# One operand for the last 16 keys of a head pair, eight theta matmuls for the last 64 tokens, and their copies on ScalarE

## Chip, cores and metric

The kernel runs on one core of a Trainium2 chip. The metric is the device time of one execution in microseconds; the median of several runs is quoted, and one further execution was taken with the hardware profiler.

## What is computed

The reference has three stages over a batch of 8, with 8 heads, 576 tokens and 64 dimensions a head (512 channels). The first is attention with keys and values averaged over groups of 8 tokens, so 72 keys a head. The second mixes tokens with a rotation by theta = x @ w_theta and ends with a channel step. The third is an ordinary token and channel MLP.

```python
k_p = k.reshape(B, H, Sp, pool, D).mean(axis=3)      # Sp = 72, pool = 8
v_p = v.reshape(B, H, Sp, pool, D).mean(axis=3)
attn = softmax(scale * q @ k_p.T)
x = attn @ v_p                                       # heads side by side: [8, 576, 512]
theta = x @ w_theta
y = w_tok_r @ (x * cos(theta)) + w_tok_i @ (x * sin(theta))
u = x + y
x = u + relu(u @ w_ch)
# then two MLPs, over tokens (256 wide) and over channels (1536 wide)
```

## The kernel before

**Precision.** Matrix products run on `F32R` operands. A value that must keep its precision is split in a high part (`h`, rounded to F32R) and a low part (`l`, the rest), and a product is the sum of high x high, low x high and high x low. `HL3` (L61) lists the three.

**Loops.** The first half of the kernel goes through the batches. While TensorE does the token mix of batch `b` (`mix_steps`, 72 steps of three matmuls each, results `m`), the work of batch `b + 1` is woven in: scores (`emit_sc`), normalisation (`emit_norm`), transposes of the probabilities (`emit_pt`), attention times value (`emit_av`), theta of the first half of the channels and of the last 64 tokens (`emit_theta`), and the products with cosine and sine (`emit_z`). `interleave` (L793) places each of these pieces at a due time from the table `P`, on a clock `clk` that adds up the columns of the matmuls emitted so far; `later` delays the work of VectorE and ScalarE behind a matmul on the same clock. So fewer matmuls in the woven part move the due pieces to an earlier place among the main matmuls. After that a list scheduler settles the order on each engine. Batch 0 goes through a plain fp32 path of its own in `emit_av` and `emit_theta`; batches 1 to 7 go through the split path.

**Last 16 keys.** A head pair has 2 x 72 keys. 128 of them go through `pt` and `vbh`/`vbl`. The 8 that are left of each head, 64 over all heads, are collected in `pl`, transposed once for all pairs (`emit_pt` with p = 4) and kept in `t1`: rows 0 to 63 high, rows 64 to 127 low. Their values are masked to the head pair: `vlh` holds the high values for both row halves, `vll` the low values for rows 0 to 63 and zeros below. So a pair and a stretch of tokens (256 or 320, `TH`) takes five matmuls in `emit_av` (L635): three with `pt`, one with `vlh` and one with `vll`.

**Last 64 tokens.** Theta of tokens 512 to 575 is computed once for cosine and sine: `dup_tail` (L535) copies the last 64 columns of `Xh`, `Xl` and `R` behind themselves on VectorE, and the 128 columns 512 to 639 are the stationary operand of 12 matmuls of 512 columns (`emit_theta` with g = 2, L696). Rows 64 to 127 of the result give the sine, rows 0 to 63 the cosine. One ScalarE activation adds a large constant that rounds (`magic`), VectorE takes the fraction (L718), ScalarE evaluates the sine, and the product goes to `zt`.

**Buffers.** `emit_theta` takes PSUM banks `t0` and `t1` by turns, and the working tiles `tmp0` and `tmp1` by turns; the tail, group 0 and group 1 of theta follow each other, so the tail and group 1 share a working tile and a bank. Attention times value uses four banks `x`, the token mix two banks `m`, freed by the addition into `R` (L789).

**Raw values.** `load_vl` (L389) brings the values of the last keys into both halves of `vlr` in two DMAs, and `prep_vl` (L427) sums over 8 tokens on VectorE, rounds on ScalarE, and builds `vlh` and `vll` on POOL. Batch 1 gets them in `pool_vl` by a matmul instead.

Of the kernel before, what the change touches and what calls it, by code (L numbers as in the profile page):

```python
# [64 lines left out]
def tile_attn_moe(  # L65
# [109 lines left out]
    con = st("con", [128, 136], F32)  # L175
    ident = con[:, 0:128]
    mask = con[:, 128:136]
    magic = st("magic", [128, 1], F32)
# [175 lines left out]
    vlh = st("vlh", [128, 4, 2, 64], F32R)  # L354
# [8 lines left out]
    def open_vlo():  # L363
        vlo["b"] = st("vbl", [128, 4, 128], F32R)
        vlo["l"] = st("vll", [128, 4, 2, 64], F32R)
        for t in vlo.values():
            nc.gpsimd.memset(t.bitcast(F32), 0.0)
# [59 lines left out]
    def prep_vl(b):  # L427
        vr = vlr_t.pop(b)
        vs = st("vls", [128, 64], F32)
        vh = st("vlsh", [128, 64], F32R)  # L430
# [4 lines left out]
        m3 = mask.unsqueeze(2)  # L435

        def fin():
            nc.gpsimd.tensor_sub(out=vs, in0=vs, in1=vh.bitcast(F32))
            nc.gpsimd.tensor_tensor(
                out=vlh.rearrange("p a e d -> p (a e) d"),  # L440
                in0=m3.to_broadcast([128, 8, 64]),
                in1=vh.bitcast(F32).unsqueeze(1).to_broadcast([128, 8, 64]),
                op=ALU.mult,
            )
            nc.gpsimd.tensor_tensor(
                out=vlo["l"][0:64].rearrange("p a e d -> p (a e) d"),
                in0=m3[0:64].to_broadcast([64, 8, 64]),
                in1=vs[0:64].unsqueeze(1).to_broadcast([64, 8, 64]),
                op=ALU.mult,
            )  # L450

        fin()
# [54 lines left out]
    def pool_vl(b):  # L507
# [5 lines left out]
        def masked(o, pr):  # L513
            nc.vector.tensor_tensor(
                out=o[pr].rearrange("p a e d -> p (a e) d"), in0=v[pr],
                in1=mask[pr].unsqueeze(2).to_broadcast([64, 8, 64]), op=ALU.mult,
            )

        lo, up = slice(0, 64), slice(64, 128)
        if b == 0:  # L520
            masked(vl0, lo)
            return
        tm = st("kr", [128, 4, 2, 64], F32, "vlt")
        vll = vlo["l"]
        masked(tm, lo)
        masked(vlh, up)
        nc.scalar.copy(out=vlh[lo], in_=tm[lo])
        nc.gpsimd.tensor_sub(out=vll[lo], in0=tm[lo], in1=vlh[lo].bitcast(F32))
# [9 lines left out]
    def emit_sc(b, p):  # L538
        q = q_t[b, p // 2][:, p % 2, :]
        if p == 0:  # L540
            e_t[b] = st("e", [128, 5, 8, 72], F32)
            pl_t[b] = st("pl", [128, 5, 2, 8, 8], F32)
# [17 lines left out]
    def emit_norm(b, p):  # L560
# [11 lines left out]
        for h in range(2):  # L572
            left = e[:, :, 2 * p + h, 64 * h:64 * h + 8]
            nc.gpsimd.tensor_copy(
                out=pl_t[b][:, :, :, 2 * p + h, :],
# [3 lines left out]
    def emit_pt(b, p):  # L579
# [4 lines left out]
        else:  # L584
            pt = st("t1", [128, T], F32R if b else F32)
            t1_t[b] = pt
        for c0, c1 in ((0, 2), (2, 5)):
# [3 lines left out]
            for c in range(c0, c1):  # L591
                if p < 4:
                    src = e[:, c, 2 * p:2 * p + 2, :].rearrange("p h k -> p (h k)")[:, 8:136]
                else:
                    src = pl_t[b][:, c].rearrange("p a h k -> p (a h k)")
# [3 lines left out]
            if b == 0:  # L599
                o, i = (pt[:, t0:t0 + n], ps[:, 0:n]) if p < 4 else (pt[0:64, t0:t0 + n], ps[0:64, 0:n])  # L600
                (nc.scalar.copy if c0 else nc.vector.tensor_copy)(out=o, in_=i)
# [12 lines left out]
    xh = {}  # L614

    def emit_av(b, j, th):
        t0, n = TH[th]
        ts = slice(t0, t0 + n)
        if j == 0 and th == 0:
            r_t[b] = st(f"R{b % 2}", [128, 4, TD], F32)  # L620
            if b > 0:
                xh[b] = (st("Xh", [128, 4, TD], F32R), st("Xl", [128, 4, TD], F32R))
        need(f"pt{j % 2}", "t1", "vbl")
# [1036 lines left out]
```

## Time and profile before

| | us |
|---|---|
| median of 3 runs (1312.93 to 1313.25) | 1313.01 |
| profiled execution | 1310.61 |
| its span on the core | 1308.7 |
| TensorE matmuls busy | 1262.2 |
| VectorE busy | 970.5 |
| ScalarE busy | 637.1 |
| POOL busy | 325.8 |

The span runs from the first to the last instruction of the profiled execution. Busy times of TensorE count pipelined matmuls with their modelled ends, so the distance between two starts is what one of them takes from the engine. The prologue fills the first 105 us or so; then the batches follow at about 60 us each until 545 us; the channel step and the two MLPs take the rest.

### The profile page before, as it was taken

To read this page: it belongs to the slowest core of one execution; us is meant where nothing else is said; L and a number is where in the kernel's file an instruction comes from. 1 tells how busy PE (TensorE), PEld (TensorE's weight loads), DVE (VectorE), ACT (ScalarE), POOL (GpSimd) and SP (SyncE) were. 2 spreads that over 40 slices of the span, in tenths; PEclk is the share of its full clock that TensorE was granted. 3 is DMA by queue.
4 is the path that set the end of the run, shared out by engine and by line. 5 is a ranking of instruction groups with operands and counts; after the bars stand their busy time and mean duration, and the time that the engine had idled before them with its cause. 6 is when DMAs were issued, how large, how long until landed. Compare 5 with 4: busy or idle time off the path is not lost.

```text
span 1308.7 us, 22307 instructions
## 1 busy us (share of the span) xinstructions
PE 1262.2 (96%) x8216; PEld 1211.6 (93%) x8216; DVE 970.5 (74%) x1749; ACT 637.1 (49%) x1190; POOL 325.8 (25%) x340
## 2 busy tenths in 40 slices
PE   6899999999999998999999999999999999999998
PEld 3588999999999998999999998999999999999998
DVE  7988576675859598587765778897555499988894
ACT  4775455545555645243332346665445454444442
POOL 4653324242324244211110002320000031223122
PEclk9999999999999999999999999999999999999999
DMA  9423221222212123446684278885437976557621
GB/s 337 148 79 115 68 95 68 96 80 84 94 61 75 35 74 125 134 171 221 236 300 182 98 262 296 279 278 195 145 134 244 357 259 224 155 159 223 184 95 66
DMA packets 119612, 213.70 MB, mean 163 GB/s; under 512 B 11152, under 2 KB 65936, under 8 KB 119504
## 3 DMA queue, kind: packets, MB, share of 16 engines
q1 hardware_dynamic: 119504, 212.29, 48.3%
q8 instruction: 64, 1.05, 0.3%
q14 instruction: 44, 0.36, 0.1%
HBM read 133.60 MB, written 78.64 MB: 162 GB/s over the span
## 4 chain that ended last, share of the span: by engine, by line
PE 69%; DVE 20%; DMA 3%; issue 3%; ACT 2%; POOL 1%; SPq 0%; DVEq 0%; ACTq 0%; POOLq 0%
PE x L159 25%; PE m L159 21%; PE t L159 20%; PE x L173 2%; DVE sm L564 2%; DVE e L553 2%; DVE mx L552 2%; DVE tmp L736 1%; DVE sm L565 1%; DMA ws<-w_ch 1%; DVE pt L605 1%; DVE R L789 1%; DVE early L261 1%; DMA scr_x<-u 1%; DVE sums L398 1%
## 5 line engine op out<-in xcount | busy, mean ns | idle before, releaser
L159 PE MATMUL m<-wtk,Z 128*128 128x256 f32 (+1 forms) x1536 | 245.0, 298 | 8.4 <-DVE R L789 6.4
L159 PEld LDWEIGHTS m<-wtk,Z 128*128 128x128 f32 x1536 | 216.0, 188 | 11.5 <-DVE R L789 6.6
L751 POOL TENSOR_TENSOR Z<-tmp,Z 128x1024 fp32r<-128x1024 f32 x31 | 76.3, 2462 | 109.4 <-ACT Z L750 109.4
L159 PE MATMUL x<-ope_Z,wa 128*128 128x384 f32 x492 | 94.8, 336 | 0.0
L1382 POOL TENSOR_TENSOR o<-o,u 128x384 f32<-128x384 f32 x12 | 16.3, 1382 | 286.1 <-DVE u L1370 195.7
L159 PEld LDWEIGHTS x<-ope_Z,wa 128*128 128x128 f32 x492 | 86.3, 188 | 0.1
L1016 POOL TENSOR_TENSOR wsum<-wm 128x128 f32<-128x128 f32 (+1 forms) x18 | 15.1, 837 | 270.0 <-DVE wm L1006 262.4
L159 PE MATMUL t<-wth,Xh 128*128 128x256 f32 (+1 forms) x504 | 76.3, 293 | 0.5 <-DVE Xh L536 0.2
L159 PEld LDWEIGHTS t<-wth,Xh 128*128 128x128 f32 x504 | 66.9, 188 | 4.5 <-DVE Xh L536 1.8
L718 DVE SCALAR_TENSOR_TENSOR tmp<-tmp,t 128x512 f32<-128x512 f32 x40 | 27.3, 683 | 53.5 <-ACT tmp L705 53.5
L736 DVE TENSOR_TENSOR tmp<-x,tmp 128x1024 f32<-128x1024 f32 x32 | 39.1, 1220 | 31.2 <-ACT tmp L712 16.1
L159 PE MATMUL x<-bdk,q 128*128 128x144 f32 x320 | 47.8, 303 | 11.6 <-DVE bdk L1441 7.1
L159 PEld LDWEIGHTS x<-bdk,q 128*128 128x128 f32 x320 | 44.7, 204 | 13.9 <-issue 11.2
L159 PE MATMUL m<-wtk,zt 128*128 128x256 f32 (+1 forms) x192 | 56.6, 295 | 0.0
L705 ACT ACTIVATE tmp<-t,magic 128x512 f32<-128x512 f32 x40 | 27.3, 683 | 54.6 <-PE t L159 42.9
L569 POOL TENSOR_TENSOR e<-e,sm 128x720 f32<-128x720 f32 x32 | 45.0, 1406 | 31.6 <-DVE sm L568 31.1
L558 ACT ACTIVATE e<-e 128x720 f32<-128x720 f32 x32 | 25.7, 804 | 51.1 <-DVE e L553 51.0
L159 PE MATMUL t<-ope_Z,wa 128*128 128x384 f32 x234 | 48.1, 336 | 1.9 <-ACT p L1290 1.9
L789 DVE TENSOR_TENSOR R<-m,R 128x256 f32<-128x256 f32 (+1 forms) x64 | 28.7, 450 | 26.8 <-PE m L159 26.8
L159 PE MATMUL m<-ope_Z,wa 128*128 128x384 f32 x234 | 48.0, 336 | 0.0
L159 PE MATMUL x<-ope_R,wa 128*128 128x384 f32 x228 | 44.1, 338 | 0.3 <-DVE p L1295 0.2
L159 PE MATMUL t<-wth,Xl 128*128 128x256 f32 (+1 forms) x252 | 43.4, 294 | 0.0
(401 smaller groups left out, 3545.3 us busy)
## 6 DMA issues: line engine op xcount, KB each, us to landing
wa<-scr_w SPq DMA_DIRECT2D x42, 512.0 KB, 5.4
scr_g<-g SPq DMA_DIRECT2D x108, 192.0 KB, 2.9
scr_w<-wo SPq DMA_DIRECT2D x42, 256.0 KB, 3.0
scr_u<-R SPq DMA_DIRECT2D x32, 288.0 KB, 2.1
u<-scr_u SPq DMA_DIRECT2D x32, 288.0 KB, 3.9
scr_w<-wo SPq DMA_DIRECT2D x18, 512.0 KB, 3.4
scr_x<-u SPq DMA_DIRECT2D x32, 288.0 KB, 2.1
raw_n<-scr_x SPq DMA_DIRECT2D x24, 384.0 KB, 3.8
```

The lines of the kernel that those rows point to most:

```text
L159: nc.tensor.matmul(out=o, lhsT=l, rhs=r, start=start, stop=stop, skip_group_check=skip)
L173: nc.tensor.transpose(o, i, ident)
L552: nc.vector.tensor_reduce(out=mx[:, c0:c1, :], in_=v, axis=AX.X, op=ALU.max)
L553: nc.vector.tensor_tensor(out=e[:, c0:c1, 2 * p:2 * p + 2, :], in0=v, in1=mx[:, c0:c1, :].unsqueeze(3).to_broadcast([128, n, 2, 72]), op=A ...
L558: nc.scalar.activation(out=ep, in_=ep, func=ACTF.Exp, scale=1.0 / 64.0)
L564: nc.vector.tensor_reduce(out=sm, in_=ep, axis=AX.X, op=ALU.add)
L569: nc.gpsimd.tensor_tensor(out=ep, in0=ep, in1=sm.unsqueeze(3).to_broadcast([128, 5, 2, 72]), op=ALU.mult)
L705: nc.scalar.activation(out=t, in_=pt, func=ACTF.Identity, bias=magic[:, 0:1])
L718: nc.vector.scalar_tensor_tensor(out=t, in0=t, scalar=MAGIC, in1=pt, op0=ALU.subtract, op1=ALU.subtract)
L736: nc.vector.tensor_tensor(out=tmp, in0=px.unsqueeze(1).to_broadcast([128, 2, 512]), in1=tmp, op=ALU.mult)
L751: later(1.0 if lo is nc.vector else 0.0, lambda: lo.tensor_sub(out=zl, in0=zv, in1=zh.bitcast(F32)), tg, zg)
L789: nc.vector.tensor_add(out=R[:, j, ts], in0=o, in1=R[:, j, ts])
```

## The change

**Last 16 keys.** The 64 rows of the last keys are cut in two groups of 32 (head pairs 0 and 1, pairs 2 and 3). For each group a tile of 96 rows holds probabilities as high, high, low, and a tile of values as high, low, high, so that one matmul with 96 rows makes the sum of all three products. `t1` becomes two tiles (`t1` and `n1`), each filled by a ScalarE copy of 64 rows and a VectorE subtraction of 32; `pl` is collected in the matching order; `vlh` becomes the one tile `vlt`, `vll` is used for batch 0 alone, and the masks get eight more columns. The values are loaded in 32-row pieces, three for each group, into `vlr` and `n2`.

**Last 64 tokens.** The high and the low part of the last 64 tokens stand side by side in one stationary operand `xt` (tag `n3`): its first 64 columns give high x w, its last 64 low x w. Eight matmuls (high and low part of w, four slices each) replace 12; the product of low with low is in the sum too. `fold` then adds the lower half of the rows to the upper: ScalarE copies rows 64 to 127 out, VectorE adds, and rounding and fraction go on for 64 rows only.

**Copies.** The duplicate of `R` and the two copies into `xt` run on ScalarE; the duplicates of `Xh` and `Xl` are gone.

```diff
@@ load_vl
-        t = st("vlr", [128, 512], F32)
-        nc.sync.dma_start(out=t[0:64], in_=vl[b])
-        nc.sync.dma_start(out=t[64:128], in_=vl[b])
+        t = [st(x, [128, 512], F32, "vlr") for x in ("vlr", "n2")]
+        for g in range(2):
+            for r in range(3):
+                nc.sync.dma_start(out=t[g][32 * r:32 * r + 32], in_=vl[b, 32 * g:32 * g + 32])
@@ prep_vl
-        nc.vector.tensor_reduce(
-            out=vs, in_=vr.rearrange("p (d o) -> p d o", o=8), axis=AX.X, op=ALU.add
-        )
-        nc.scalar.copy(out=vh, in_=vs)
...
+        for g in range(2):
+            nc.vector.tensor_reduce(
+                out=vs[0:96, g], in_=vr[g][0:96].rearrange("p (d o) -> p d o", o=8), axis=AX.X, op=ALU.add
+            )
+        nc.scalar.copy(out=vh[0:96], in_=vs[0:96])
+        nc.gpsimd.tensor_sub(out=vh[32:64], in0=vs[32:64], in1=vh[32:64].bitcast(F32))
...
@@ emit_pt, p = 4
-                nc.scalar.copy(out=pt[:, t0:t0 + n], in_=ps[:, 0:n])
-                lo = pt[64:128, t0:t0 + n]
-                later(P["lo"], lambda o=lo, i=ps[64:128, 0:n]: nc.vector.tensor_sub(
-                    out=o, in0=i, in1=o.bitcast(F32)), last_bank[0], "t1")
+                for g in range(2):
+                    gr = slice(64 * g, 64 * g + 32)
+                    nc.scalar.copy(out=pt[g][0:64, t0:t0 + n], in_=ps[64 * g:64 * g + 64, 0:n])
+                    later(P["lo"], lambda o=pt[g][64:96, t0:t0 + n], i=ps[gr, 0:n], h=pt[g][0:32, t0:t0 + n]:
+                          nc.vector.tensor_sub(out=o, in0=i, in1=h.bitcast(F32)),
+                          last_bank[0], ("t1", "n1")[g])
@@ emit_av
-            (vlh[:, j].rearrange("p e d -> p (e d)"), t1[:, ts]),
-            (vlo["l"][:, j].rearrange("p e d -> p (e d)"), t1[:, ts]),
+            (vlt[0:96, j].rearrange("p e d -> p (e d)"), t1[j // 2][0:96, ts]),
...
-                dup_tail(h)
-                dup_tail(l)
-                dup_tail(r)
+                for a, x in enumerate((h, l)):
+                    nc.scalar.copy(out=xt[b][:, :, a], in_=x[:, :, 512:T].bitcast(F32))
+                dup_tail(r, nc.scalar.copy)
@@ emit_theta
+            if tail:
+                for w in range(2):
+                    for k in range(4):
+                        mm(o, xt[b][:, k].rearrange("p a t -> p (a t)"), wth[k][:, w, d0:d0 + nd],
+                           n == 0, n == 7)
+                        n += 1
+                continue
...
+        if tail:
+            lo = tmp[0:64, 0, :]
+            nc.scalar.copy(out=lo, in_=pt[64:128])
+
+            def fold():
+                th = tmp[64:128, 0, :]
+                nc.vector.tensor_add(out=th, in0=pt[0:64], in1=lo)
+                nc.scalar.activation(out=t[64:128], in_=th, func=ACTF.Identity, bias=magic[64:128, 0:1])
+
+                def frac():
+                    nc.vector.scalar_tensor_tensor(
+                        out=t[64:128], in0=t[64:128], scalar=MAGIC, in1=th, op0=ALU.subtract, op1=ALU.subtract
+                    )
+
+                    def sins():
+                        nc.scalar.activation(out=t[0:64], in_=t[64:128], func=ACTF.Abs)
+                        nc.scalar.activation(out=t, in_=t, func=ACTF.Sin, scale=-TWO_PI, bias=phase[:, 1:2])
...
```

**Order on TensorE**, batch 4 beside batch 5, at the first products of attention times value (`x` is the result, `pt` and `t` the probabilities, `m` the token mix). Before:

```order
L159 MATMUL x_3792<-pt_3721,vbh 128x320
L159 MATMUL x_3792<-pt_3721,vbl 128x320
L159 MATMUL x_3784<-t_3769,vlh 128x256
L159 MATMUL x_3784<-t_3769,vll 128x256
L159 MATMUL x_3792<-pt_3721,vbh 128x320
L159 MATMUL m_3762<-wtk_552,Z_3442 128x256
L159 MATMUL x_3792<-t_3769,vlh 128x320
L159 MATMUL x_3792<-t_3769,vll 128x320
L159 MATMUL m_3762<-wtk_559,Z_3442 128x256
```

The same place now:

```order
L159 MATMUL x_3807<-pt_3731,vbl 128x320
L159 MATMUL x_3807<-pt_3731,vbh 128x320
L159 MATMUL m_3772<-wtk_552,Z_3447 128x256
L159 MATMUL x_3800<-t_3779,vlh 128x256
L159 MATMUL m_3772<-wtk_559,Z_3447 128x256
L159 MATMUL m_3772<-wtk_594,zt_3260 128x256
L159 MATMUL x_3818<-pt_3748,vbh 128x256
L159 MATMUL x_3818<-pt_3748,vbl 128x256
L159 MATMUL x_3818<-pt_3748,vbh 128x256
L159 MATMUL x_3818<-t_3779,vlh 128x256
L159 MATMUL x_3807<-t_3779,vlh 128x320
```

The `vll` matmuls are gone, a `vbh` matmul of 320 columns and a main matmul of 256 now stand ahead of the first `t` matmul, and the 320-column `t` matmul stands seven places behind it. Between the last product of attention times value and the theta tail there were three main matmuls of 256 columns and twelve of 320; there are 16 of 320 now. From the first `t` matmul to the tail the new order holds nine more main matmuls of 320 columns (21 for 12) and one fewer of 256 (20 for 21), since the tail's due time is the same and less stands before it.

**Order on ScalarE**, same batches, from the last product of attention times value to the theta tail and group 0 of theta (`t_3929`, `t_3946` are the tail's banks). Before:

```order
L645 CAST Xh<-x_3892 128x320
L646 COPY R_3780<-x_3892 128x320
L424 CAST vbh<-sums 64x2x64
L434 CAST vlsh<-vls 128x64
L705 ACTIVATE tmp_3944<-t_3929,magic 128x512
L714 ACTIVATE tmp_3944<-tmp_3944 64x512
L715 ACT_TABLE_LOAD
```

Now:

```order
L636 CAST Xh<-x_3909 128x320
L637 COPY R_3794<-x_3909 128x320
L644 CAST xt<-Xh 128x4x64
L525 COPY R_3794<-R_3794 128x4x64
L424 CAST vbh<-sums 64x2x64
L644 CAST xt<-Xl 128x4x64
L424 CAST vbh<-sums 64x2x64
L435 CAST vlsh<-vls 96x128
L706 COPY tmp_3957<-t_3946 64x512
L711 ACTIVATE tmp_3957<-tmp_3957,magic 64x512
L719 ACTIVATE tmp_3957<-tmp_3957 64x512
```

The three copies of the last tokens stand behind the last R copy, with a `vbh` cast between them, and the tail's activation has become a copy and an activation with VectorE's addition between the two.

## Rows read from the trace of the kernel before

**Rows 1.** The page's busy times with shares, and the last chain by engine.

```profile
PE 1262.2 (96%) x8216; PEld 1211.6 (93%) x8216; DVE 970.5 (74%) x1749; ACT 637.1 (49%) x1190; POOL 325.8 (25%) x340
...
PE 69%; DVE 20%; DMA 3%; issue 3%; ACT 2%; POOL 1%; SPq 0%; DVEq 0%; ACTq 0%; POOLq 0%
```

**Rows 2.** Stretches: length; busy PE, PEld, DVE, ACT, POOL; clock; DMA share; GB/s.

```profile
304.40:364.50 60.10, 58.76 (x449) 57.30 (x449) 41.41 (x81) 32.38 (x61) 20.64 (x20) 1.00 0.26 84
...
485.00:545.00 60.00, 56.27 (x424) 54.79 (x423) 39.42 (x84) 24.48 (x41) 19.34 (x13) 1.00 0.27 88
```

**Rows 3.** Groups by form: count, busy us, mean ns of one, idle before.

```profile
L159 PE MATMUL x<-t,vll 128*128 128x320 f32 x28 | 8.7, 309 | 0.0
...
L159 PE MATMUL x<-t,vll 128*128 128x256 f32 x28 | 7.9, 281 | 0.0
...
L159 PE MATMUL t<-wth,Xl 128*128 128x512 f32 x28 | 7.5, 390 | 0.0
```

**Rows 4.** Timeline, 355 to 357 us, TensorE: start, length, operation.

```profile
355.82 0.28 PE L159 MATMUL x<-t,vll 128*128 128x256 f32 x1
...
355.94 0.31 PE L159 MATMUL x<-pt,vbh 128*128 128x320 f32 x1
...
356.53 0.31 PE L159 MATMUL x<-t,vll 128*128 128x320 f32 x1
...
356.67 0.71 PE L173 MATMUL x<-con,e 128*128 128x128 f32 x5
```

**Rows 5.** Timeline of TensorE, 306 to 327 us.

```profile
306.37 1.07 PE L159 MATMUL t<-wth,Xl 128*128 128x512 f32 x4
307.27 1.10 PE L159 MATMUL t<-wth,Xh 128*128 128x256 f32 x8
...
326.43 0.86 PE L159 MATMUL m<-wtk,Z 128*128 128x256 f32 x6
```

**Rows 6.** Waits of TensorE, 105 to 560 us: total, times, longest.

```profile
PE m L159 <- DVE R L789: 6.0, 7, 1.5
PE x L159 <- DVE t L610: 2.9, 6, 1.4
```

**Rows 7.** Timeline, 352 to 355 us: making of t1 and its first matmul.

```profile
352.53 0.75 ACT L608 CAST t<-x 128x256 fp32r<-128x256 f32 x2 [1.81 <-PE x L173]
...
353.72 0.83 DVE L610 TENSOR_TENSOR t<-x,t 64x256 fp32r<-64x256 f32 x2
...
354.20 0.39 PE L159 MATMUL x<-t,vlh 128*128 128x256 f32 x1 [0.29 <-DVE t L610]
```

**Rows 8.** Timeline, 362 to 365 us: from the last evacuation to the theta tail.

```profile
362.62 0.41 ACT L645 CAST Xh<-x 128x320 fp32r<-128x320 f32 x1
...
362.94 0.42 ACT L646 COPY R<-x 128x320 f32<-128x320 f32 x1
...
363.80 0.66 DVE L536 CAST Xh<-Xh 128x256 fp32r<-128x256 f32 x1
363.84 0.60 PE L159 MATMUL m<-wtk,Z 128*128 128x320 f32 x3
...
364.52 1.69 PEld L159 LDWEIGHTS t<-wth,Xh 128*128 128x128 f32 x8 [0.34 <-DVE Xh L536]
```

**Rows 9.** Timeline of ScalarE, 307 to 323 us: theta and the high half of Z.

```profile
307.47 0.69 ACT L705 ACTIVATE tmp<-t,magic 128x512 f32<-128x512 f32 x1 [1.19 <-PE t L159]
...
316.73 0.69 ACT L705 ACTIVATE tmp<-t,magic 128x512 f32<-128x512 f32 x1 [1.40 <-POOL zt L751]
...
321.46 1.05 ACT L750 CAST Z<-tmp 128x1024 fp32r<-128x1024 f32 x1 [1.29 <-DVE tmp L736]
```

**Rows 10.** Timeline, 506 to 511 us: the first main matmuls of batch 7.

```profile
506.00 0.48 PE L159 MATMUL m<-wtk,Z 128*128 128x256 f32 x2 [1.53 <-DVE R L789]
...
506.68 4.01 POOL L751 TENSOR_TENSOR Z<-tmp,Z 128x1024 fp32r<-128x1024 f32 x1 [2.95 <-ACT Z L750]
...
510.74 0.50 PE L159 MATMUL m<-wtk,Z 128*128 128x256 f32 x2 [1.76 <-POOL Z L751]
```

More of the change, by code (lines that the diff above doesn't have):

```diff
@@ L364, in open_vlo @@
         vlo["b"] = st("vbl", [128, 4, 128], F32R)
-        vlo["l"] = st("vll", [128, 4, 2, 64], F32R)
-        for t in vlo.values():
-            nc.gpsimd.memset(t.bitcast(F32), 0.0)
+        nc.gpsimd.memset(vlo["b"].bitcast(F32), 0.0)
     q_t = {}
@@ L511, in pool_vl, with masked @@
         v = ps.rearrange("p (h d) -> p h d", h=8)
-        def masked(o, pr):
+        def masked(o, pr, m):
             nc.vector.tensor_tensor(
                 out=o[pr].rearrange("p a e d -> p (a e) d"), in0=v[pr],
-                in1=mask[pr].unsqueeze(2).to_broadcast([64, 8, 64]), op=ALU.mult,
+                in1=m[pr].unsqueeze(2).to_broadcast([pr.stop, 8, 64]), op=ALU.mult,
             )
-        lo, up = slice(0, 64), slice(64, 128)
         if b == 0:
-            masked(vl0, lo)
+            masked(vl0, slice(0, 128), mask0)
             return
         tm = st("kr", [128, 4, 2, 64], F32, "vlt")
[L524 to L528, printed above, removed]
+        masked(tm, slice(0, 96), mask)
+        nc.scalar.copy(out=vlt[0:96], in_=tm[0:96])
+        nc.gpsimd.tensor_sub(out=vlt[32:64], in0=tm[32:64], in1=vlt[32:64].bitcast(F32))
     e_t = {}
@@ L574, in emit_norm @@
             nc.gpsimd.tensor_copy(
-                out=pl_t[b][:, :, :, 2 * p + h, :],
+                out=pl_t[b][:, :, p // 2, :, 2 * (p % 2) + h, :],
                 in_=left.unsqueeze(2).to_broadcast([128, 5, 2, 8]),
@@ L584, in emit_pt @@
         else:
-            pt = st("t1", [128, T], F32R if b else F32)
-            t1_t[b] = pt
+            t1_t[b] = [st(x, [128, T], F32R, "t1") for x in ("t1", "n1")] if b else st("t1", [128, T], F32)
+            pt = t1_t[b]
         for c0, c1 in ((0, 2), (2, 5)):
@@ L599, in emit_pt @@
             if b == 0:
-                o, i = (pt[:, t0:t0 + n], ps[:, 0:n]) if p < 4 else (pt[0:64, t0:t0 + n], ps[0:64, 0:n])
-                (nc.scalar.copy if c0 else nc.vector.tensor_copy)(out=o, in_=i)
+                (nc.scalar.copy if c0 else nc.vector.tensor_copy)(out=pt[:, t0:t0 + n], in_=ps[:, 0:n])
             elif p < 4:
@@ L621, in emit_av @@
             if b > 0:
-                xh[b] = (st("Xh", [128, 4, TD], F32R), st("Xl", [128, 4, TD], F32R))
-        need(f"pt{j % 2}", "t1", "vbl")
+                xh[b] = (st("Xh", [128, 4, T], F32R), st("Xl", [128, 4, T], F32R))
+                xt[b] = st("n3", [128, 4, 2, 64], F32R, "xt")
+        need(f"pt{j % 2}", "t1", "n1", "vbl")
         pt, t1 = pt_t[b, j], t1_t[b]
@@ L679, in emit_theta @@
         else:
-            need("Xl")
+            need("Xl", "n3")
         chunks, d0, nd = theta_geo(half, g)
+        tail = g == 2 and b > 0
         if g < 2:
@@ L704, in emit_theta @@
         t = tmp[:, 1, :]
+        if tail:
[12 more added lines that the diff above has]
+                        nc.scalar.activation(out=t, in_=t, func=ACTF.Sin, scale=-TWO_PI, bias=phase[:, 1:2])
+                    later(P["sn"], sins, tg)
+                later(P["fr"], frac, tg)
+            later(P["sn"], fold, bk, tg)
+            return
         nc.scalar.activation(out=t, in_=pt, func=ACTF.Identity, bias=magic[:, 0:1])
```

42 lines of the change are left out of this document (19 added, 23 removed).

## Prediction

> **What bounds the kernel now.** I read the totals first: TensorE is busy for 96% of the span, and the chain that ended last runs over it for 69% [rows 1]. Then the stretches: one batch of the first half lasts 60.10 us, TensorE is busy for 58.76 of them, VectorE for 41.41 and ScalarE for 32.38, all at a granted clock of 1.00, which is the 2.4 GHz level [rows 2]. The list of waits is short: between 105 and 560 us TensorE waited 6.0 us in seven places for the additions into R and 2.9 us in six for `t1` [rows 6]. So a matmul taken out of a batch should come back almost whole, unless it uncovers a chain on the other engines. The batch turn is where I look for that, because all that the change touches lies there.
>
> **What it removes on TensorE.** In each of the seven batches that go through the split path, attention-times-value loses one matmul of five in each of 8 groups (four of 256 columns, four of 320), and theta of the last 64 tokens loses 4 of 12 matmuls of 512 columns. The busy times by form [rows 3] count pipelined matmuls twice over (281, 309 and 390 ns each), so I price by the distance from one start to the next. The 256-column one holds the engine from 355.82 to 355.94, 0.12 us; the 320-column one from 356.53 to 356.67, 0.14 us [rows 4]. The four `Xl` matmuls of theta hold it from 306.37 to 307.27, 0.90 us or 0.225 each [rows 5].
> - Attention-times-value: 28 x 0.12 + 28 x 0.14 = 7.3 us.
> - Theta: 28 x 0.225 = 6.3 us.
> - Together 13.6 us, 1.94 a batch. The bounds of this term are 12.5 (a start distance is rounded to 0.01 us) and 14.5.
>
> The Trainium skill ("TensorE: Matmul & The Clock Gate", section "Wait — 56ns, not 53.3ns?") gives N ÷ 2.4 GHz plus about 2.5 ns for back-to-back matmuls. By it, as an estimate, 256, 320 and 512 columns cost 109, 136 and 216 ns and the term would be 12.9 us, 0.7 less; the rows run some 5% slower than that, and the sum keeps the rows.
>
> **What it adds beside that path.** These have one answer each, so they go together. ScalarE casts `t1` in four pieces where it had two (0.75 us for the pair now [rows 7]; +0.75), takes three copies of the last tokens and one copy of half a theta. VectorE subtracts `t1` in four pieces (0.83 for the pair [rows 7]; +0.83), reduces the last values in two pieces, adds one theta fold, and loses three copies. With 19 us of VectorE and 28 us of ScalarE idle in a batch [rows 2], some 2 us more of either costs nothing by itself. The load of the last values becomes six DMAs instead of two on SyncE, each small; they stand after the next batch's `kr` load and before stores of `u`, and what they carry is wanted a batch later. The POOL work gets shorter. In batch 0 several of these reductions and loads are ordered earlier than before, among the evacuations; that is one place, not seven, and I give it 0 with 1.5 us either way.
>
> **Two waits that it moves.** First `t1`. TensorE now stops 0.29 us before the first `t` matmul [rows 7]. In the new order two matmuls (320 and 256 columns) stand ahead of that point that stood behind it, 0.26 us of work, so the wait is nearly filled. The first of the four subtractions still starts when the addition into R is done and is as long as before, since both are 256 columns wide. The third, which is the one for 320 columns, ends about 0.8 us after the first, and TensorE asks for it only after seven more matmuls of 0.12.
>
> Second, the theta tail. Now the engine is through with its matmuls at about 363.84 + 3 x 0.147 = 364.28 and starts the tail at 364.52, so 0.24 us are lost to the copy of `Xh` [rows 8]. In the new order all eight tail matmuls need both copies into `xt`, and these stand in ScalarE's queue behind the last R copy, with the R duplicate and one `vbh` cast between them. After the last product ScalarE needs about 0.2 to start, 0.32 for Xh, 0.42 for R [rows 8], and then four pieces that cost between 0.25 (start to start) and 0.42 (the whole of the longer R copy) each: ready after 1.9 to 2.6 us. TensorE has 16 matmuls of 320 columns to do there, 16 x 0.147 = 2.35 us, where it had three short and twelve long. So the wait is 0 to 0.25; I take 0.1, against 0.24 now. The two waits together give back about 0.3 us in each of the five plain turns; I take 1.2 us in all, with 0 and 2.7 as ends.
>
> **The last turn gives some back.** Where batch 7 begins, conversions of later weights fill VectorE, and TensorE already waits for them: 1.53 us for a bank, then 1.76 for the low half of Z, which POOL finishes at 510.69 [rows 10]. That chain starts from the theta tail and does not get shorter with fewer matmuls. TensorE would reach it earlier by the 0.9 us of theta and by about 1.3 us for the nine main matmuls that are now ordered ahead of the tail, 2.2 in all. The chain may start some 0.8 us sooner, because the transposes for the tail do. I take 1.4 us lost, between 0 and 2.2.
>
> **The sum.** 13.6 + 1.2 - 1.4 = 13.4 us. The profiled execution took 1310.61 us for a span of 1308.7, so it would take 1297.2. The median of the runs shown is 1313.01, 2.4 above it; the whole difference lies within the span, so I carry it over unchanged: **1299.6 us**.
>
> **Rivals.**
> - *Everything is regained.* The waits go and the last turn hides its chain: 13.6 + 2.7 - 0 = 16.3, so 1296.7. For it: the new order puts work before both waits. Against: the 1.76 us wait at batch 7 is already a chain's end.
> - *New waits at the tail.* `xt` comes late, or the second main group of theta finds its bank still held by the fold (ScalarE's copy, then VectorE's addition; I count the addition done 4.3 us after the tail begins and the bank wanted at 4.6, so 0.3 us of margin). The price is 0.5 to 1.1 us a turn, 7 x 0.8 = 5.6: 13.6 - 1.4 - 5.6 = 6.6, so 1306.4; with a smaller price 1303. For it: both margins are under half a microsecond, and ScalarE's queue is in order. Against: nothing in it is more than one copy too long. The Trainium skill ("ScalarE: Activation LUTs", section "Rules for kernel authors") advises VectorE rather than ScalarE for plain elementwise work because VectorE is faster per element; by it the three copies would stay where they were. That bears on this rival alone, and its price above needs no figure of the page.
> - *Slower: the chain of Z sets every turn.* The theta tail and the third group of theta share a buffer, so ScalarE begins the third group's theta at 316.73, after POOL's work on the tail, and its high half of Z is ready at 321.46 + 1.05 = 322.5; the next batch's first main matmuls come at 326.43 [rows 5, 9]. That is 3.9 us of cover; the change takes about 2.2 of it away, so 1.7 remain. The fold puts a copy and an addition into that chain (now one 0.69 us activation [rows 9]), but the tail waits for TensorE's transposes today, which come 0.9 sooner. It decides from a chain 1.7 us later than that; beyond it each microsecond costs seven, and to end 0.2% slower it must come 4 us later: 13.4 - 7 x 2.3 = -2.7, so 1315.7.
> - *No change.* VectorE's normalisation in the middle of a batch sets the period (the chain gives VectorE 20% [rows 1], and the additions into R hold TensorE for 6.0 us). Against: that stage lies before the stretch that is shortened, in every batch, and TensorE is idle for only 1.3 us of the 60. About 1312.
>
> **How the numbers follow.** The forecast (1297.6 to 1302) gets 0.56, everything regained 0.15, new waits 0.21 (half of it up to 1305), no change 0.04, slower 0.04. A measurement of this kernel tells about 0.2%, 2.6 us, from no change. The likeliest gives 1299.6; 1296.0 to 1305.0 leaves out some 0.19. Faster is 0.92, same 0.04, slower 0.04.
>
> **What the profile after would show.** The period of a plain batch falls from 60.1 to about 58.0; five turns give 2.1 us each and the last one about 0.6. The groups with `vll` are gone, the theta tail is one group of 56 matmuls of 512 columns. TensorE's waits name ScalarE's `xt` with less than 0.3 us a turn. Near the start of batch 7 the waits for R and Z grow from about 3.5 to about 5 us in all. It would be wrong if TensorE waited half a microsecond or more for `xt` or for the fold's addition in each turn, or if Z's POOL work became a wait in the plain batches.

## The result, and the profile after

| us | before | after |
|---|---|---|
| median of 4 runs each, one chip | 1312.97 (1311.92 to 1313.25) | 1301.86 (1300.99 to 1303.75) |
| profiled execution, its span | 1310.61, 1308.7 | 1303.75, 1302.0 |
| mean granted clock in it | 1.000 | 0.993 |

The ratio is 0.9919, with a 95% interval of 0.9902 to 0.9936: faster, by 11.1 us at the median. The forecast was 1299.6 us, and 1301.86 lies in its range of 1296.0 to 1305.0. The two profiled executions are only 6.7 us of span apart, because the one of before was quicker than any of the four runs beside it and the one of after is the slowest of its four; what lies behind that is a large part of what follows.

The page of the changed kernel, the lines that answer to [rows 1], and the row of the granted clock in 40 slices:

```profile
PE 1252.8 (96%) x8130; PEld 1205.6 (93%) x8132; DVE 977.4 (75%) x1754; ACT 653.7 (50%) x1232; POOL 321.7 (25%) x339
...
PEclk9899999999999998999999999999999999999999
...
PE 70%; DVE 14%; DMA 3%; issue 2%; ACT 1%; SPq 0%; POOL 0%; DVEq 0%; ACTq 0%; POOLq 0%
```

TensorE still sets the end. The clock row has an 8 in two slices, where before it had 9 throughout. The same stretch of a plain batch as in [rows 2], from theta tail to theta tail (busy time of PE, PEld, DVE, ACT, POOL; clock; DMA share; GB/s):

```profile
301.21:359.29 58.08, 57.05 (x440) 55.69 (x438) 44.32 (x86) 34.85 (x68) 19.96 (x20) 1.00 0.27 87
```

60.10 us have become 58.08, TensorE's idle time is 1.0 us (1.3 before), and VectorE and ScalarE took on 2.9 and 2.5 us. In the groups by form the `vll` groups of [rows 3] are gone; these are two of the new ones:

```profile
L159 PE MATMUL t<-wth,xt 128*128 128x512 f32 x56 | 14.5, 401 | 0.0
...
L159 PE MATMUL x<-t,vlh 96*128 96x320 f32 x28 | 8.7, 312 | 0.0
```

The waits of TensorE between 105 and 560 us, as in [rows 6]:

```profile
PE m L159 <- DVE R L812: 6.4, 7, 1.7
PE m L159 <- ACT Z L773: 3.0, 1, 3.0
PE x L173 <- DVE u L901: 1.8, 1, 1.8
PE x L159 <- DVE t L600: 1.2, 1, 1.2
```

`t` is now waited for once, in batch 7, where [rows 6] have it six times; neither `xt` nor the fold's bank appears. TensorE now waits 3.0 us for ScalarE's high half of Z, where it waited 1.8 us for POOL's low half, and 1.8 us for `u` after the last turn, where it waited 0.2.

**Where the time went.** I cut each profiled span at three marks that every kernel has: A is the start of the theta tail at the turn from batch 1 to 2, B the mean of the five turns after it, C the time from the last tail to the last eight transposes of R in batch 7, and D the rest, so the span is A + 5 B + C + D. The forecast's steps go to these parts as follows: A loses 2.98 (batch 1's 1.94 and 1.04 of batch 2) and gains 1.3 for the main matmuls that now stand ahead of the tail; B loses 1.94 and 0.24; C loses 0.9 and 1.3 and gains 1.4.

| us | A | B | C | D | span |
|---|---|---|---|---|---|
| before | 184.54 | 59.99 | 33.71 | 790.5 | 1308.7 |
| by the forecast's steps | 182.9 | 57.81 | 32.9 | 790.5 | 1295.3 |
| after | 185.21 | 58.03 | 34.92 | 791.7 | 1302.0 |
| `after_again` | 184.99 | 58.02 | 34.89 | 791.2 | 1301.2 |
| `before_again` | 187.07 | 59.95 | 33.78 | 790.3 | 1310.9 |
| `av_only` | 185.46 | 58.86 | 34.51 | 790.3 | 1304.6 |
| `theta_only` | 185.77 | 59.42 | 33.21 | 791.4 | 1307.5 |
| `copies_dve` | 184.36 | 57.99 | 34.22 | 792.0 | 1300.5 |
| `b0_old` | 182.83 | 58.00 | 33.81 | 792.5 | 1299.1 |
| `conv_act` | 184.48 | 58.00 | 33.10 | 789.7 | 1297.3 |
| `b0_conv` | 182.45 | 58.04 | 32.93 | 791.9 | 1297.4 |
| `b0_conv_dve` | 184.03 | 58.19 | 32.28 | 790.0 | 1297.3 |
| `b0_conv_warm` | 183.47 | 58.01 | 32.38 | 791.2 | 1297.1 |
| `warm` | 195.03 | 58.06 | 32.80 | 792.4 | 1310.5 |
| `conv_late` | 184.67 | 57.84 | 27.83 | 814.4 | 1316.1 |

The plain turns came nearly as forecast. The profiled execution lost 2.3 us in A, 1.1 over the five turns, 2.0 in C and 1.2 in D against the forecast's steps: 6.7 us in all. The experiments go by these parts. A differs between executions of one kernel too (184.54 and 187.07 us for the kernel before), so a difference in A between two single profiles can mislead by as much.

### The profile page after: what moved, and what is told of

The parts are those of the page before. It is cut to its first block, busy times and chain, and to the rows that moved or that the text cites. A ratio compares the mean times of both kernels' runs of the same rounds, so it can differ in the third digit from the quotient of the medians.

```text
span 1302.0 us, 22269 instructions
## 1 busy us (share of the span) xinstructions
PE 1252.8 (96%) x8130; PEld 1205.6 (93%) x8132; DVE 977.4 (75%) x1754; ACT 653.7 (50%) x1232; POOL 321.7 (25%) x339
## 4 chain that ended last, share of the span: by engine, by line
PE 70%; DVE 14%; DMA 3%; issue 2%; ACT 1%; SPq 0%; POOL 0%; DVEq 0%; ACTq 0%; POOLq 0%
PE x L159 24%; PE m L159 24%; PE t L159 20%; PE x L173 2%; DMA ws<-w_ch 2%; DVE sm L553 1%; DVE e L542 1%; DVE mx L541 1%; DVE tmp L759 1%; DVE sm L554 1%; DMA scr_x<-u 1%; DVE R L812 1%; DVE pt L593 1%; DMA scr_w<-wo 0%; DVE p L1314 0%
## 5 line engine op out<-in xcount | busy, mean ns | idle before, releaser
L159 PE MATMUL m<-wtk,Z 128*128 128x256 f32 (+1 forms) x1536 | 253.8, 301 | 9.4 <-DVE R L812 6.4
L159 PEld LDWEIGHTS m<-wtk,Z 128*128 128x128 f32 x1536 | 220.0, 191 | 12.4 <-DVE R L812 8.1
L159 PE MATMUL t<-wth,Xh 128*128 128x256 f32 x448 | 61.8, 279 | 0.0
L159 PE MATMUL x<-bdk,q 128*128 128x144 f32 x320 | 47.9, 303 | 12.9 <-DVE bdk L1464 7.3
L159 PEld LDWEIGHTS t<-wth,Xh 128*128 128x128 f32 x448 | 57.0, 188 | 0.9 <-DVE tmp L710 0.2
L741 DVE SCALAR_TENSOR_TENSOR tmp<-tmp,t 128x512 f32<-128x512 f32 x33 | 22.5, 683 | 32.2 <-ACT tmp L728 32.2
L773 ACT CAST Z<-tmp 128x1024 fp32r<-128x1024 f32 x32 | 33.3, 1042 | 20.4 <-DVE tmp L759 20.4
L159 PE MATMUL m<-ope_Xl,wa 128*128 128x384 f32 x204 | 42.6, 336 | 0.6 <-ACT ope_Xl L1152 0.6
L159 PEld LDWEIGHTS t<-ope_Z,wa 128*128 128x128 f32 x234 | 41.4, 188 | 1.8 <-ACT p L1313 1.8
```

The lines of the kernel that those rows point to most:

```text
L159: nc.tensor.matmul(out=o, lhsT=l, rhs=r, start=start, stop=stop, skip_group_check=skip)
L741: nc.vector.scalar_tensor_tensor(out=t, in0=t, scalar=MAGIC, in1=pt, op0=ALU.subtract, op1=ALU.subtract)
L773: nc.scalar.copy(out=zh, in_=zv)
```

## Experiments

Medians are each beside runs of the kernel before on the same chip (1314.94, 1313.84 and 1314.21 us in the three sets); the ratio is to those.

### Either part alone

`av_only` is the changed kernel with the last 64 tokens as before, the three duplicates on VectorE included:

```diff
...
-        tail = g == 2 and b > 0
+        tail = False
```

`theta_only` is the kernel before with the `xt` operand, the fold and the copies on ScalarE.

> Only the one-operand part for the last 16 keys (and with it the new masks and the 128-row probabilities of batch 0); the last 64 tokens are treated as in the kernel before, with 12 matmuls and three VectorE copies. Theory (TensorE time comes back whole in the plain batches, but batch 0 ends with a longer stop on TensorE and a fallen clock, and that comes with this part): 7.3 us of matmuls and about 0.6 us of t1 waits come back, about 2 us are lost before 110 us, so 1307 us against 1313, with a granted clock below 1 near 55 us and full clock near 500 us. Rival (the loss before 110 us belongs to the theta part or to chance): 1305 us and a full clock throughout.

Measured: 1307.13 us (1305.51 to 1311.5), ratio 0.9949 (0.9932 to 0.9965).

> Only the eight-matmul theta of the last 64 tokens, with its copies on ScalarE; the last 16 keys and batch 0 are as in the kernel before. Theory (the last turn loses the gain of this part): 6.3 us of matmuls and about 0.6 us of waits come back, batch 0 stays as it was, and the turn into batch 7 loses 2 to 3.5 us by a longer wait for Z and a fallen clock behind it: about 1309 us, full clock near 55 us, below 1 near 500 us. Rival (the last turn is lost only where both parts shorten TensorE's work): 1306 to 1307 us and a full clock throughout.

Measured: 1309.50 us (1308.12 to 1311.31), ratio 0.9962 (0.9947 to 0.9977). The two gains, 0.51% and 0.38%, add up to 0.89%, about what the whole change gives (0.81% and, below, 0.86%). In the plain turns B falls by 1.13 us with the first part, where 1.04 of matmuls and the 0.3 of the wait for `t` should have gone, and by 0.57 with the second, where 0.90 of matmuls and 0.24 of a wait should have gone. The waits of TensorE from 125 to 450 us in `theta_only` show most of the reason for the second:

```profile
PE t L159 <- ACT xt L655: 1.8, 5, 0.6
...
PE x L159 <- DVE t L610: 1.5, 5, 0.3
```

0.36 us a turn, of the 0.57 that are missing, go to ScalarE's copy into `xt`. That is the forecast's rival of new waits at the tail, and it is real where the theta part stands alone. Together with the first part, 16 main matmuls stand before the tail, and they cover the copies. Both expectations had the granted clock wrong in one place: `av_only` has the halved clock behind its wait for Z as well (0.50 from 503 to 506 us), and `theta_only` also near 57 us. The longer stop in batch 0, however, came with `av_only` and not with `theta_only`.

### The copies' engine

```diff
-                    nc.scalar.copy(out=xt[b][:, :, a], in_=x[:, :, 512:T].bitcast(F32))
-                dup_tail(r, nc.scalar.copy)
+                    nc.vector.tensor_copy(out=xt[b][:, :, a], in_=x[:, :, 512:T].bitcast(F32))
+                dup_tail(r)
```

> The changed kernel with the three copies of the last tokens on VectorE instead of ScalarE. Theory (the copies lie beside 16 matmuls of 2.35 us and cost nothing on either engine): 1301 to 1303 us, the wait of TensorE at the theta tail under 0.3 us a turn in both. Rival 1 (ScalarE's queue delays the operand, VectorE is quicker): 0.1 to 0.3 us a turn gained, 1300 us. Rival 2 (VectorE's queue is the tighter one there): 0.3 us or more lost in each turn, 1304 us or more.

Measured: 1301.92 us (1301.36 to 1302.29), ratio 0.9904 (0.9889 to 0.9919): the same as the changed kernel. TensorE waits for neither in the first four plain turns. In the changed kernel the timelines of ScalarE and then of TensorE show how close it is (start, length, operation):

```profile
358.80 0.40 ACT L644 CAST xt<-Xl 128x256 fp32r<-128x256 f32 x1
```

```profile
359.29 2.07 PE L159 MATMUL t<-wth,xt 128*128 128x512 f32 x8
361.19 1.10 PE L159 MATMUL t<-wth,Xh 128*128 128x256 f32 x8
362.13 0.64 PE L159 MATMUL t<-wth,Xl 128*128 128x256 f32 x4
```

`xt` is ready at 359.20, 2.26 us after TensorE leaves the last product of attention times value (356.94), and TensorE asks for it at 359.29. The first four turns of `copies_dve` were 0.13 to 0.28 us shorter (57.71 to 57.95, against 57.92 to 58.08), with the same order on TensorE. Its rows behind the tail:

```profile
357.81 2.01 PE L159 MATMUL t<-wth,xt 128*128 128x512 f32 x8
359.66 1.07 PE L159 MATMUL t<-wth,Xh 128*128 128x256 f32 x8
360.57 0.64 PE L159 MATMUL t<-wth,Xl 128*128 128x256 f32 x4
```

Eight matmuls of 256 columns hold TensorE for 0.91 us here and for 0.94 there, eight of 512 for 1.85 and 1.90, at a granted clock of 1.00 in both. So I took the difference for the matmul rate of those executions, and tried the same pair once more on another base (`b0_conv`, below; the list that the next expectation speaks of is `after_again`, `b0_conv`, `b0_conv_dve`, `b0_conv_warm`).

> As the kernel before it in this list, and the three copies of the last tokens on VectorE. Theory (where the copies run makes no difference, since 16 matmuls cover them; the 0.24 us a turn by which they looked quicker on VectorE were TensorE's matmul rate in that execution, 0.91 against 0.94 us for eight): within 0.7 us of the kernel with the copies on ScalarE. Rival (VectorE is the quicker engine for them): 1.2 us faster, and the plain turns 0.24 us shorter at the same matmul rate.

Measured: 1299.18 us (1297.68 to 1300.75), beside 1299.23 with the copies on ScalarE. The first four turns were 57.94 to 58.06 us with VectorE and 57.91 to 58.06 with ScalarE (one of 58.57 aside, where two theta matmuls stand ahead of the tail). A copy takes 0.28 us on VectorE and 0.40 on ScalarE in these turns. That VectorE is the quicker agrees with the rule of the Trainium skill that the forecast cites ("ScalarE: Activation LUTs", section "Rules for kernel authors"), although the rule names relu, max, min, add and mul and not copies. It earns nothing here, since 16 main matmuls cover either. In the median the engine of the copies makes no difference.

In the fifth turn, the one into batch 7, it does. VectorE is full of weight conversions there, two of its three copies take 0.7 to 0.8 us, and TensorE stops in `copies_dve`, as it does in `b0_conv_dve`:

```profile
474.29 1.88 PE L159 MATMUL t<-wth,xt 128*128 128x512 f32 x7 [0.93 <-DVE xt L644]
```

That turn is 58.65 and 58.99 us long, against 58.00 and 57.74 with the copies on ScalarE, and C is 0.7 us shorter in both pairs (34.92 to 34.22, 32.93 to 32.28), so most of what the stop costs comes back there.

### The kernel before and the changed kernel again

> The kernel before, unchanged, to see the spread between executions and the granted clock in each. Theory: 1312 to 1313 us with the clock at 1.000 or close to it in every execution, so that the fallen clock belongs to the changed kernel. Rival: its clock falls in most executions too (0.99), and the profiled one, 2.4 us quicker than the median, was an exception; then the clock explains little of the difference between the kernels.

Measured: 1312.84 us (1309.81 to 1315.57, 12 runs), ratio 0.9991 (0.9980 to 1.0001). The rival was right: its clock is between 0.994 and 0.997 in each of these executions. In the profiled one (span 1310.9, mean clock 0.995) it is half in stretches that begin at 64, 85 and 105 us and at 798. Five us around the end of the first one, with the mean clock in the last column but two:

```profile
65.00:70.00 5.00, 5.00 (x22) 4.18 (x21) 4.93 (x9) 4.99 (x11) 2.19 (x4) 0.73 0.00 0
```

Its A is 187.07 us, 2.5 more than in the profile that the forecast was read from, with the same plain turns; the sixteen products of 256 columns at 63.72 us take 5.41 us there and 3.72 in the other. The 2.4 us between that profile and the median, which the forecast carried over as a constant, are probably this for the most part.

> The changed kernel, unchanged, on the same chip as the three below. Theory: 1301 to 1303 us with the stop of 5.8 us for R in batch 0, waits of 4.7 us at the turn into batch 7 and a halved clock behind both, as these came in every kernel with the 128-row form of batch 0. Rival (they were one execution's accident): a profile without one of them, and 1299 to 1300 us.

Measured: 1302.40 us (1301.28 to 1302.99), ratio 0.9914 (0.9898 to 0.9931). The 5.8 us stop, the waits of 4.7 us and the halved clock behind both are all there again, so they belong to the kernel, though not all of them to the change: the kernel before drops its clock in the prologue as well.

### Batch 0

In A the changed kernel stops for R in batch 0, 5.8 us where it was 3.1; the end of the row is the wait, and the last column but two of the second row is the clock:

```profile
56.56 5.71 PE L159 MATMUL t<-wt,R 128*128 128x512 f32 x9 [5.80 <-DVE R L525]
```

```profile
55.00:60.00 5.00, 3.44 (x4) 1.51 (x5) 5.00 (x10) 3.08 (x8) 3.83 (x6) 0.50 1.04 329
```

`b0_old` gives batch 0 back its 64-row form, and leaves the rest of the change:

```diff
...
-            mm(o, vl0[:, j].rearrange("p e d -> p (e d)"), t1[:, ts], False, True)
+            mm(o, vl0[0:64, j].rearrange("p e d -> p (e d)"), t1[0:64, ts], False, True)
```

> The changed kernel with batch 0's last keys as in the kernel before: 64 rows of probabilities and values, copied and multiplied as 64 rows. Theory (batch 0's end is set by VectorE's and POOL's conversions, and the 128-row form only lets TensorE arrive earlier and changes who collides there): the stop for R is about 3 us as before and the main products begin 0 to 1 us earlier, 1301 to 1302 us; what the 128-row form saves on TensorE (0.3 us a product group, 2.4 us in all) was never on the path. Rival (that saving is real): 1303 to 1304 us.

Measured: 1301.19 us (1299.55 to 1303.04), ratio 0.9902 (0.9886 to 0.9919). The stop is 3.1 us again and A is 182.83, the forecast's 182.9, although the clock is half twice in it (from 55.7 and 83.0 us on). The stop goes with the form in every profile: 3.1 us in all seven with 64 rows, 5.8 in all six with 128 rows and no idle work in the stop. What it costs is less certain. This pair of profiles says 2.4 us; A is 182.45 to 184.03 in four changed kernels with 64 rows and 184.36 to 185.21 in five with 128, 1.5 us apart on average; between medians it is 0.7 to 1.2 us, with overlapping intervals. POOL shows the link: its timeline in the changed kernel,

```profile
37.82 2.63 POOL L226 TENSOR_SCALAR early<-early 128x288 f32<-128x288 f32 x2 [1.65 <-ACT early L225]
40.64 2.06 POOL L226 TENSOR_SCALAR early<-early 128x288 f32<-128x288 f32 x1 [0.19 <-ACT early L225]
42.66 1.91 POOL L226 TENSOR_SCALAR cvt<-cvt 128x288 f32<-128x288 f32 x1
```

and in `b0_old`:

```profile
37.25 1.18 POOL L226 TENSOR_SCALAR early<-early 128x288 f32<-128x288 f32 x2 [1.64 <-ACT early L225]
40.08 0.43 POOL L226 TENSOR_SCALAR early<-early 128x288 f32<-128x288 f32 x1 [1.65 <-DVE early L268]
40.51 0.46 POOL L226 TENSOR_SCALAR cvt<-cvt 128x288 f32<-128x288 f32 x1
```

The same four steps of weight conversion take 2.07 us of POOL in one and 6.60 in the other. VectorE has 0.15 us of idle time just before 37.73 in `b0_old`, waiting for TensorE's transposes, and none from 37 to 44 us in the changed kernel, where TensorE is ahead. All seven profiles with the 64-row form have such a gap and the short steps, and all with the 128-row form have no gap and the long ones. That the missing gap is what holds POOL was not tried by itself. From POOL the delay goes to ScalarE's part of the conversions,

```profile
45.38 0.47 ACT L223 ACTIVATE early<-early_w 128x288 f32<-128x288 f32 x1 [3.42 <-POOL wtk L296]
```

and from there, as far as the order of the work tells, to the last copies of R and so to TensorE. The Trainium skill ("GPSIMD Engine Reference", section "1. Specifications") says that POOL shares its SBUF interfaces with VectorE and contends with instructions that have two SBUF inputs or use both ports; VectorE runs instructions with two inputs back to back there (0.45 us each), and the trace agrees that POOL is held; the size, 0.43 us become 2.06, is the trace's.

### The last turn

TensorE in the changed kernel, at the first main matmuls of batch 7, beside [rows 10]:

```profile
490.46 1.44 PE L159 MATMUL m<-wtk,Z 128*128 128x320 f32 x8 [1.71 <-DVE R L812]
...
498.03 1.65 PE L159 MATMUL m<-wtk,Z 128*128 128x256 f32 x6 [2.99 <-ACT Z L773]
...
501.61 1.91 PE L159 MATMUL m<-wtk,Z 128*128 128x256 f32 x8
```

The waits sum to 4.7 us, against 1.53 and 1.76 in [rows 10], 3.7 with two short ones beside them. The last row is the surprise: eight matmuls of 256 columns hold the engine for 1.71 us (to 503.32) and not 0.94, at the 1.2 GHz level. Two kernels move the conversions of weights, to test whether these set this chain, and one adds idle work, to test the clock.

`conv_act` gives one of five VectorE steps of the last turn's conversions to ScalarE:

```diff
-    "md": (1.7, 2.0),
+    "md": (1.0, 2.0),
```

> The changed kernel with one of the five VectorE steps of each weight conversion in the last turn (the absolute value) given to ScalarE. Theory (VectorE's conversions hold the chain that makes batch 7's Z: 2.6 us between ScalarE's last sine and VectorE's product): the waits for R and Z near 488 to 498 us fall from 4.7 to about 3 us and 1 to 2 us are gained, 1300 to 1301 us. Rival (the chain is ScalarE's and POOL's; more on ScalarE delays it): 1302 us or more.

Measured: 1300.10 us (1299.13 to 1301.12), ratio 0.9893 (0.9877 to 0.9908). Beside 1301.86 and 1302.40 for the changed kernel the gain came, but the step named for it did not: the waits are 4.5 us (4.0 for Z, 0.5 for R), and Z's high half is ready 22.3 us after the tail begins, where it took 22.6. What fell is the time at the lower clock, by half, and D (by 2.0 us, in an execution that was the quickest of its four). VectorE's queue is still held in that chain, as in the kernel before (2.47 us in place of 0.35 at 500.12) and in the changed kernel:

```profile
491.36 2.46 DVE L249 TENSOR_SCALAR cvt<-stg 128x192 uint32<-128x192 uint32 x1
```

0.25 us is what the same step takes elsewhere. POOL's work on the low half of Z runs from 491.16 to 493.70, so this looks like the contention of batch 0 the other way round; in the kernel before POOL works on Z from 499.98 to 502.38.

`conv_late` lets the last turn's conversions work in the memory of `Xh` alone, which the last theta releases, and moves their due times behind that theta:

```diff
...
-                    vr = st("vr", [128, 3, CV], F32, "late1")
+                    vr = st("Xh", [128, 5, CV], F32, "late1")
...
-                           (["cvt0", "vlr"] + [vr[:, i] for i in range(3)])[0:1 + n[1]])
+                           [] + [vr[:, i] for i in range(5)])
```

> The changed kernel with the conversions of the last turn working in the memory of Xh, so that they can't begin before the last theta of batch 7 has read it (about 505 us). Theory (these conversions cause the waits for R and Z at the last turn, and the fallen clock behind them): the 4.7 us of waits shrink to under 1.5, the clock stays up, 4 to 6 us are gained there, and some is given back near 545 us where the channel step wants the weights: 1296 to 1300 us. Rival (all of it is given back there, since 35 us of conversions then press into 40 us): 1302 us or more.

Measured: 1318.53 us (1315.70 to 1321.46), ratio 1.0038 (1.0025 to 1.0051). The first half of the theory holds: TensorE waits 0.8 us for Z there, the clock stays up, and C is 27.83 us, 7.1 less. What is given back was far larger than thought:

```profile
PE m L159 <- ACT Xh L887: 19.5, 1, 19.5
```

The channel step waits 19.5 us for memory that the conversions still hold, and D is 814.4 us. So the conversions do cause the waits of the last turn, and in the place tried here there is no room behind it. All engines' part of the conversions moved in this kernel, so it does not say that VectorE's is what counts.

`warm` puts idle work into both stops:

```diff
+        if b == 0 and half == 0 and g == 2:
+            for _ in range(9):
+                nc.tensor.matmul(out=pt[:, 0:320], lhsT=vb0[:, 3, :], rhs=pt_t[0, 3][:, 256:576], start=True, stop=True)
...
+            if b == B - 1 and half == 0 and jj == 0 and th == 0:
+                keep_busy(hold["ps"], 12)
```

> The changed kernel with idle work for TensorE in its two long stops: nine repeats of batch 0's last fp32 product (320 columns, 0.54 us each, 4.8 us) in the stop of 5.8 us for R near 51 us, and twelve bf16 products of 512 columns (some 2.6 us) ahead of batch 7's first main product, where it stops 3.0 us for Z. Theory (the clock that falls to its lower level in these stops costs time after them: 3.6 us of matmuls at half speed near 57 us, 5.6 us near 498): 2 to 4 us gained, 1298 to 1300 us, with the granted clock at 1.00 in both stretches. Rival (the time after the stops is set by the other engines, or the clock falls anyway): 1301.5 us or more.

Measured: 1311.01 us (1309.59 to 1313.20), ratio 0.998 (0.997 to 0.999). As a whole it failed: the scheduler put ScalarE's first theta work of batch 0 behind more conversions, and TensorE then stood 10.3 us (A is 195.03). In the last turn it did what it should. The clock stays at 1.00, C is 32.80 us against 34.92, and the waits for Z shrink to what the idle work leaves. The matmuls behind the high half of Z begin 22.69 us after the tail in `warm` and 22.68 in the changed kernel, so the whole difference lies behind the wait. The 2.0 us that C lost against the forecast are therefore the clock's.

### Together

`b0_conv` joins `b0_old` and `conv_act`; `b0_conv_warm` adds sixteen idle products ahead of batch 7's first main matmul.

> The changed kernel with batch 0's last keys in 64 rows again, and the absolute value of the last turn's conversions on ScalarE. Theory (the two losses are separate places, so their gains add up: 0.7 to 2 us from batch 0, 1.8 us from the last turn): 1298 to 1299.5 us, faster than the changed kernel. Rival (the gain of either was spread between executions): 1300.5 us or more.

Measured: 1299.23 us (1298.63 to 1300.84), ratio 0.9894 (0.9877 to 0.9911); 3.2 us below `after_again` on the same chip, so the gains add up, as the theory had it.

> As the second kernel in this list, with sixteen bf16 products of 512 columns (3.5 us) on TensorE ahead of batch 7's first main product, where it stops 4 us for Z. Theory (part of the last turn's loss is the clock that halves behind that stop): the clock stays at 1.00 near 500 us, and 1 to 1.5 us are gained against the second kernel, 1297 to 1298.5 us. Rival (the time behind the stop is set by POOL's low half of Z): no gain, although the clock stays up.

Measured: 1297.63 us (1295.94 to 1301.58), ratio 0.9880 (0.9860 to 0.9900). The waits of C shrink from 4.5 us to 1.6, beside the idle work, and the clock stays up there:

```profile
491.11 3.63 PE L169 MATMUL m<-busy 128*128 128x512 bf16 x16
494.39 0.59 PE L159 MATMUL m<-wtk,Z 128*128 128x256 f32 x2
495.88 0.97 PE L159 MATMUL m<-wtk,Z 128*128 128x256 f32 x6 [0.90 <-ACT Z L774]
```

C is 32.38 us. The median is 4.8 us below the changed kernel's on that chip and the best of all here, though its slowest run (1301.58) lies among the changed kernel's. Against `b0_conv` the 1.6 us are not certain: the runs overlap, and C is only 0.6 us shorter in the profiles.

## Why the prediction was right, and where it was off

**TensorE is the bound, and matmuls come back whole: right.** Its busy share stayed at 96%, and B fell by 1.96 us.

**The term of 1.94 us a batch: right for the matmuls that went, but a turn gave a little less.** The tail's eight matmuls took 1.90 us from 359.29 on, where twelve took 2.85 from 304.42 on, so theta gave 0.95 for the 0.90. With the waits, the sum has 2.18 us a plain turn (its last paragraph rounds to 2.1), and 1.96 came, although the waits gave back more than the 0.24 taken: 0.3 for `t` and 0.24 for `Xh` are both gone. The two rates of TensorE do not explain the 0.22. At 0.94 us for eight the kernel before has turns of 60.06 to 60.17 us and the changed one of 58.06 to 58.08, some 2.0 apart. What the starts on TensorE show is that the new order has more places where one matmul holds the engine some 0.08 us longer than others of its width (from 0.04 to 0.13). A plain turn ahead of the last has 13 of them before (1.2 us in all), 19 in `av_only` (1.65) and 21 in the changed kernel (1.8), 12 of these among the products of attention times value between 347 and 356 us, like this one, where the next start comes after 0.19 us and not 0.12:

```profile
355.43 0.35 PE L159 MATMUL x<-pt,vbh 128*128 128x256 f32 x1
355.62 0.29 PE L159 MATMUL x<-t,vlh 96*128 96x256 f32 x1
```

The forecast has no term for these 0.6 us, and no run shows what makes them. The rule of the Trainium skill ("TensorE: Matmul & The Clock Gate", section "Wait — 56ns, not 53.3ns?"), cited in the forecast for 12.9 us, gives 109 ns for 256 columns; the rows of both kernels have 114 and 118, and the measurement decides.

**Work beside that path costs nothing: right in the batches, wrong in batch 0.** The six DMAs, the fold and the copies show in no wait of the plain turns. "0 with 1.5 us either way" for batch 0 is the step that failed: A came 2.3 us late against the profile that the forecast was read from, whose clock did not drop, and some 1.5 of it goes with the 128-row form in the profiles. I had looked for the price in the reductions and loads that are ordered earlier. It is in the 128-row form, which brings TensorE forward in a stretch that VectorE, ScalarE and POOL bound, and beside which the same work on POOL takes three times as long. Against the other profile of the kernel before (187.07) A fell by 1.9 us, about the 1.7 forecast, so part of the 2.3 is the quiet base.

**The two waits: right in direction, and more came back than was taken.** `xt` was ready 2.26 us after the last product (1.9 to 2.6 forecast) against 2.35 us of matmuls. `theta_only` shows how little was to spare.

**The last turn: right in its mechanism, short by the clock.** The chain of Z did not get shorter (its high half came 22.2 us after the tail before, 22.6 now) and TensorE reached it 2.2 us sooner; the waits grew to 4.7 us, about 5 forecast. That the longer stop would halve the clock behind it was not in the forecast, and is worth about 2 us (C 34.92, and 32.80 with the clock up, 32.9 forecast).

**What comes after: missed.** D is 0.7 to 1.2 us longer in the two profiles of the changed kernel. VectorE there waits 2.04 us, 0.49 before, for a weight block that came 6.6 us earlier (550.34 for 556.97) where TensorE came 8.2 us earlier (550.64 for 558.80); TensorE's 1.8 us for `u` follow from that. No experiment isolated it, and D lies between 789.7 and 792.5 us in all the other kernels here but `conv_late`.

**The median: a fortunate sum.** Against the profile's own forecast of 1297.2 us the profiled execution was 6.5 us slow; against 1299.6 the median was 2.3. The constant carried from profile to median probably stood for halved-clock stretches that the profile of before happened not to have. It covers 2.4 of the 6.5 us, and another 1.9 are gone because the profiled execution was that much above its own median; that the median came so close is in part luck.

## What to carry to other kernels

Here the removed matmuls came back nearly whole in the steady loop, which TensorE bounds (1.96 us of 2.18 a turn); look for the loss where TensorE isn't the bound, at the prologue and at the last turn, because arriving earlier there only lengthened a stop here. Price such a stop with what the clock does behind it, and cover it with idle work if it can't be removed. Before a profile is taken as a base, compare its granted clock with other executions: one that never drops may be the exception.

## What the hardware showed that was not expected

- **The clock halves behind stops, and not only there.** In the changed kernel it is at the 1.2 GHz level from about 53 to 60 us and from 497 to 504 us, each time beginning within a stop of TensorE. It also drops at 77 us, where TensorE has been busy since 70.23, behind 24 products of 16 columns (73.79 to 76.75 us) that ran at 1.00 themselves. In the first profile of the kernel before the same products (72.96 to 75.92 us) were not followed by a drop.
- **TensorE has two rates at a granted clock of 1.00.** Eight matmuls of 256 columns take 0.91 or 0.94 us, whole stretches at a time, changing within a batch and from batch to batch, in every kernel. No run here shows what sets it.
- **A product with 64 rows was slower than with 128.** In batch 0 the fp32 product of 64 rows and 256 columns holds TensorE for 0.63 us, the one of 128 rows for 0.43:

```profile
35.42 0.70 PE L159 MATMUL x<-t,vl 64*128 64x256 f32 x2
36.05 0.61 PE L169 MATMUL x<-busy 128*128 128x512 bf16 x2
```

```profile
34.83 0.60 PE L159 MATMUL x<-t,vl 128*128 128x256 f32 x2
35.26 0.59 PE L169 MATMUL x<-busy 128*128 128x512 bf16 x2
```

The weight load beside it begins with the product there, at 35.42, and ahead of it here, at 34.72. Most matmuls of 96 rows in the batches show no such loss: they follow at 0.12 us like those of 128.
- **A step on VectorE or POOL can take five to ten times as long beside work of the other:** 0.43 us became 2.06 on POOL, and 0.25 became 2.46 on VectorE.
